# Paced weight swaps: 16 loads per segment tied to steps of TensorE's program

## The chip, the cores and the metric

The kernel runs on one core of one Trainium2 chip. The metric is the device time of one execution in microseconds, taken as the median of several runs. The engines are TensorE (PE, with its weight loads as PEld), VectorE (DVE), ScalarE (ACT), GpSimd (POOL) and SyncE (SP). SyncE computes nothing here; it issues almost all transfers, one after the other, in the order of its own program, and a transfer that has to wait holds up all that stand behind it on that queue.

## What is computed

Two parts are added with a gate per token. Part A is a recurrent attention over 64 segments of 32 tokens with 8 memory rows; part B is a gated feed-forward layer. Cut to the core:

```python
# x: (1, 2048, 640) bf16; H = 32 heads of Dh = 192; M = 8 memory rows; seg_len = 32
for s in range(64):
    h = concat([mem, x[32 * s:32 * s + 32]])            # 40 rows
    q, k, v = h @ Wq, h @ Wk, h @ Wv                    # 640 -> 32 x 192 each
    p = softmax(mask(q @ k.T * Dh ** -0.5))
    o = (p @ v) @ Wo                                    # 6144 -> 640
    mem, a[s] = o[:8], o[8:]
b = (gelu(x @ w_gate) * (x @ w_up)) @ w_down
out = g * a + (1 - g) * b                               # g = sigmoid(sum(x * gate_w))
```

Segment s + 1 needs the memory rows that segment s makes at its very end, so the segments follow one another strictly, and in each all four weight matrices are used once.

## The kernel before

**Tiles and stages.** Part B comes first, in four blocks of 512 tokens (about the first 170 us); then come the 64 segments. In a segment the 32 heads are worked in four *octets* of eight heads. Weights lie in the on-chip memory as *pieces*: a piece of Wq, Wk or Wv is one of five slices of the contraction (k = 0 to 4) for one octet, 128 rows of 3072 bytes, 384 KB; a piece of Wo is one pair of heads' pairs, 128 rows of 3840 bytes, 480 KB. A segment reads 60 pieces of the first sort and 16 of Wo.

**What does not fit is swapped.** All four matrices together are larger than the memory, so 16 slots hold two pieces in turn: 13 slots hold a Q, K or V piece of octet 0 or of octet 3 (`partner`, NSQ = 13), three hold a Wo piece of the first or of the last pairs (NSW = 3). Even segments go through the octets 0, 1, 2, 3, odd ones 3, 2, 1, 0. So a slot's first piece is read at the start of a segment, and its other piece has to be there toward the end of the same segment; the next segment then starts with what lies there. The 16 loads of a segment thus have a window from the read that frees the slot to the read of the other piece. One further piece of Q (k = 2) is read from a copy, and its slot is loaded at a fixed step late in the segment.

**The order of the work is written out by hand.** `PROG0` to `PROG3` (from L528) list the steps of a segment for s % 4 = 0, 1, 2, 3, called its *kind* below. `("g", n, k)` is a step of projections: slice k of the pieces of group n (L1152, and L226 for a piece that goes with the same loaded rows). Group 0 reads Q and K of the segment's first octet, group 1 its V and the second octet's Q and K, and so on; groups 3, 4 and 5 read Q, K and V of the last octet. `("sc", i)` are scores (mask at L1201), `("ex", i)` softmax, `("pt", i)` the transposes of P, `("pv", i)` P times V (L1296, L1298), `("wo", i, j)` the output projection (L1352 and L1378; L1397 in segments of kind 3), `("lf", ...)` and `("le", ...)` projections of the last 8 rows of four later segments, made ahead (L944), and `("vb", k)` V of such rows.

**Who issues what.** `segment(s)` (L1476) walks through the list; after each step it calls `swap_loads` (L664, called at L1529). That function takes the keys of the pieces just read, and for each that has a partner adds the partner's load to SyncE's program at once (`load_piece`, L647; its transfers show as L649), with a wait on the last reader of the slot. K pieces of slices 2 and 3 of the first group are held until the Q pieces of slices 3 and 4 have been added. After `swap_loads`, at fixed steps, the small transfers are added to the same queue:

- at ("g", 0, 3): the store of left rows of an earlier segment (L955); in kind 0 also the out store of the last segment (`out_store`, L1043)
- at ("g", 1, 4): in kinds 1 to 3 the out store; in all the load of the next segment's x (L757); in kind 0 four stores of left rows into the output (`outl_store`, L1086), in kind 2 four loads into the same buffer (`bzl_load`, L1038)
- in kind 1, at the first ("le", ...): the store of the first half of left rows (`mid_store`, L1433)
- at ("wo", 0, 1): in kind 1 the second half of those rows (L1433); the load of part B's rows (`bz_load`, L1032), which waits until the out store has landed; in kind 1 also a load of left x (`xl_load`, L761)
- at ("pv", 2): two staging loads of left rows (`stg_load`, L1019; in kind 1 the second is issued later), the load of the Q piece with k = 2, and in kinds 0 and 2 four more of L1086 or L1038.

`_Sched.add` (L73) finds each operation's dependencies from the memory regions that it reads and writes; an out store and a left-row store of the same segments write overlapping rows of the output, so the later one waits for the earlier one's landing.

Of the kernel before, what the change touches and what calls it, by code (L numbers as in the profile page):

```python
# [238 lines left out]
def _build(nc, A_x, A_mem0, A_Wq, A_Wk, A_Wv, A_Wo, seg_len, w_gate, w_up, w_down,  # L239
# [34 lines left out]
    S_ = _Sched(nc)  # L274
# [238 lines left out]
    def piece_src(key):  # L513
        if key[0] == 3:
            return Wo2[:, key[1]]
        m, o_, k = key
        return (Wq2, Wk2, Wv2)[m][:, k, OW * o_:OW * (o_ + 1)]
# [4 lines left out]
    def piece_view(key, o):  # L522
        if key[0] == 3:
            return bview(o, GO).rearrange("p (c n) -> p c n", n=Dm)
        return bview(o, GQ)

    GROUPS = [[(0, 0), (1, 0)], [(2, 0), (0, 1), (1, 1)], [(2, 1), (0, 2), (1, 2)], [(2, 2), (0, 3)], [(1, 3)], [(2, 3)]]
# [46 lines left out]
    def octet(s, i):  # L574
        return i if s % 2 == 0 else NOCT - 1 - i
# [67 lines left out]
    later = []  # L643

    loaded = {}

    def load_piece(key, name):  # L647
        loaded[slot_id[key]] = key
        S_.add("sp", lambda e: e.dma_start(piece_view(key, res_off[key]), piece_src(key)), writes=[r_res[key]],  # L649
               dma_sem="slot%d" % slot_id[key], name="%s %s" % (name, key))  # L650

    def piece(seg, key):
        order = orders[seg % 4]
        oi = last_req.get(seg, -1) + 1
        assert order[oi] == key, "pieces must be consumed in order"
        last_req[seg] = oi
        if seg == 0 and key in tmp_off:
            return left_piece(key)
        if seg and key == (EM, octet(seg, 0), EK):
            return None, None  # L660
        done_keys.append(key)
        return piece_view(key, res_off[key]), r_res[key]

    def swap_loads(seg, item):  # L664
        if item[:2] == ("g", 0) and EK <= item[2] < KT - 1:
            later.extend(key for key in done_keys if key[0] == 1)
            done_keys[:] = [key for key in done_keys if key[0] != 1]
        elif later:
            done_keys[:] = sorted(done_keys + later, key=lambda key: key[:1] + key[2:])
            del later[:]  # L670
        for key in done_keys:
            other = swap_in.get(key)
            if other is None or (other in partner) == (seg % 2 == 0):
                continue
            load_piece(other, "swap s%d" % seg)
        del done_keys[:]

    def left_piece(key):
        if key in tmp_off:
            return piece_view(key, tmp_off[key]), r_tmp[key]  # L680
        return piece_view(key, res_off[key]), r_res[key]
# [448 lines left out]
    def proj(s, item):  # L1130
# [25 lines left out]
        for n, (m, i) in enumerate(group_at(item)):  # L1156
            o, bk = octet(s, i), bk_of[(m, i)]
            g_, rg_ = piece(s, (m, o, k))
            S_.add("pe", mms(m, bk, htile(k), k, g_, n > 0),
                   reads=([rg_] if rg_ else r_ek) + [r_Hm[int(k >= KA[1])], r_HxT], writes=[r_ps[bk]],  # L1160
                   name="%s s%d o%d k%d" % ("QKV"[m], s, o, k))
# [206 lines left out]
    def wo_part(s, item):  # L1368
        ub = item[1] % NUB
        u = uT[ub]  # L1370
        pairs = wo_pairs(s, item)
        lasto = item[1] == NOCT - 1
        allp = wo_pairs(s, ("wo", NOCT - 1)) if lasto else [p for i in range(NOCT - 1) for p in wo_pairs(s, ("wo", i))]
        held = [(p,) + piece(s, (3, p)) for p in pairs]
        if lasto:
            for p, g_, rg_ in held:
                for c in range(3):
                    S_.add("pe", [lambda e, j=j, c=c, g_=g_, p=p: e.matmul(  # L1378
                        ps[32 * j:32 * j + 32, OB2, SC:512], u[:, p % 4, c, 0:L], g_[:, c, DJ * j:DJ * (j + 1)],
                        start=(p == allp[0] and c == 0), stop=(p == allp[-1] and c == 2),  # L1380
                        tile_position=(0, 32 * j)) for j in range(4)],
                        reads=[rg_, r_uTh[p % 4 // 2]], writes=[r_ps[OB2]], name="Wo s%d p%d" % (s, p))
            return
        for (pa, ga, ra), (pb, gb, rb) in zip(held[::2], held[1::2]):
            for c in range(3):
                S_.add("pe", wo_split(OB, [u[:, pa % 4, c, 0:L], u[:, pb % 4, c, 0:L]], [ga[:, c, :], gb[:, c, :]],
                                      pa == allp[0] and c == 0, pb == allp[-1] and c == 2),
                       reads=[ra, rb, r_uT[ub]], writes=[r_ps[OB]], name="Wo s%d p%d" % (s, pa))
        if pairs[-1] == allp[-1]:
            half_copy(OB, "s%d" % s)  # L1390

    def wo_both(s, item):
        for p in wo_pairs(s, item):
            g_, rg_ = piece(s, (3, p))
            u, ru = (U3h[p % 4 // 2][:, p % 2], r_U3h[p % 4 // 2]) if item[1] == NOCT - 1 else (U3[:, p % 4], r_U3)
            for c in range(3):
                S_.add("pe", [lambda e, i=i, g_=g_, c=c, p=p, u=u: e.matmul(  # L1397
                    ps[64 * i:64 * i + 64, LB, 0:2 * DJ], u[:, c, :], g_[:, c, 2 * DJ * i:2 * DJ * (i + 1)],
                    start=(p == NWP - 1 and c == 0), stop=(p == 0 and c == 2), tile_position=(0, 64 * i),
                    skip_group_check=True) for i in range(2)],  # L1400
                    reads=[rg_, ru], writes=[r_ps[LB]], name="Wb s%d p%d" % (s, p))
# [74 lines left out]
    def segment(s):  # L1476
# [3 lines left out]
        for n, item in enumerate(PROGS[q]):  # L1480
# [43 lines left out]
            else:  # L1524
                if q == 3:
                    wo_both(s, item)
                else:
                    wo_part(s, item)
            swap_loads(s, item)  # L1529
            if item == ("g", 0, KT - 2):  # L1530
                for x in to_store:
# [109 lines left out]
def bass_gated_mix__memory_aug_recurrent_mem_tr__glu_gated_geglu__prompt_kernel(  # L1641
    nc,
    A_x,
    A_mem0,
    A_Wq,
    A_Wk,
    A_Wv,
    A_Wo,
    A_seg_len,
    B_x,  # L1650
    B_w_gate,
    B_w_up,
    B_w_down,
    gate_w,
    out,
):
    _build(nc, A_x, A_mem0, A_Wq, A_Wk, A_Wv, A_Wo, A_seg_len, B_w_gate, B_w_up, B_w_down, gate_w, out)
# [33 lines left out]
```

## Time and profile before

| | us |
|---|---|
| median of three runs | 1701.26 |
| lowest, highest | 1691.61, 1701.76 |
| the profiled execution | 1693.53 |
| its span, first to last instruction | 1691.8 |
| TensorE busy | 1555.9 |
| VectorE, ScalarE, GpSimd busy | 985.0, 780.1, 549.0 |
| all transfers | 499.30 MB |

The span is what the trace shows of the profiled execution; times of rows are counted from its start. In the profile's rows a group of instructions is named by its line, engine, operation, what it writes and reads, and its count; then come busy time and mean of one, and the idle time of the engine just before, with what ended most of it. In a row of the timeline stand start, duration, engine, line, operation, and in brackets idle time before it. The on-chip memory is one tile, `arena`, and the accumulators one, `ps`, so rows are told apart by their lines and by the matrix that a transfer reads. An issue row of SyncE gives when the issue began and how long issuing took, for several issues of one line together if they follow each other; how long a transfer takes to land is a separate answer.

### The profile page before, as it was taken

How to read it: one execution, taken by the hardware profiler on the slowest of the kernel's cores; microseconds unless marked ns; L12 is line 12 of the kernel's file. 1: busy time of each engine (PE TensorE's matmuls, PEld its weight loads, DVE VectorE, ACT ScalarE, POOL GpSimd, SP SyncE). 2: the span in 40 equal slices, each digit the busy share in tenths (PEclk: the TensorE clock that was granted, in tenths of full speed). 3: DMA queues.
4: the chain of work that ended last, by engine and by line, in shares of the span. 5: the costliest groups of instructions: out<-in, count | busy, mean ns of one | idle time of the engine just before them, and what ended most of it. 6: DMA issues, size and time to landing. Idle time of an engine off the chain costs nothing.

```text
span 1691.8 us, 76086 instructions
## 1 busy us (share of the span) xinstructions
PE 1555.9 (92%) x37107; PEld 775.0 (46%) x28147; DVE 985.0 (58%) x3039; ACT 780.1 (46%) x1890; POOL 549.0 (32%) x1625
## 2 busy tenths in 40 slices
PE   9999989999989989899999899898989899898986
PEld 4444345444444445454444444454534444454443
DVE  6452656666555656566665656555665556565663
ACT  2222444544445554455444554444544445445442
POOL 1100233333333333333333333333333333233332
PEclk9999999999999999999999999999999999999998
DMA  9915988988889898889889897889888898889895
GB/s 297 334 47 161 356 293 308 331 311 290 306 298 328 298 325 298 304 314 327 305 291 324 290 338 277 305 296 317 312 296 311 281 330 295 278 297 320 300 329 188
DMA packets 275418, 499.30 MB, mean 295 GB/s; under 512 B 121119, under 2 KB 136327, under 8 KB 275079
## 3 DMA queue, kind: packets, MB, share of 16 engines
q1 hardware_dynamic: 271000, 491.30, 83.5%
q8 instruction: 255, 4.18, 1.0%
q10 hardware_dynamic: 4079, 3.14, 0.6%
q14 instruction: 84, 0.69, 0.1%
HBM read 473.25 MB, written 21.09 MB: 292 GB/s over the span
## 4 chain that ended last, share of the span: by engine, by line
PE 62%; DMA 28%; SPq 4%; DVE 3%; issue 2%; ACT 1%; POOL 0%; DVEq 0%; ACTq 0%; POOLq 0%
PE ps L1152 18%; PE ps L226 16%; DMA arena<-in_A_Wo_dram 13%; DMA arena<-in_A_Wk_dram 11%; PE ps L1397 7%; PE ps L1352 4%; DMA arena<-in_A_Wv_dram 4%; PE ps L1296 3%; PE ps L944 2%; PE ps L1201 2%; PE ps L1378 2%; SPq L649 2%; PE ps L853 2%; PE ps L850 2%; PE ps L876 1%
## 5 line engine op out<-in xcount | busy, mean ns | idle before, releaser
L1152 PE MATMUL ps<-arena 128*32 128x384 bf16 x8640 | 653.9, 331 | 35.2 <-DMA arena<-in_A_Wk_dram 15.9
L226 PE MATMUL ps<-arena 128*32 128x384 bf16 x8960 | 642.2, 329 | 0.4 <-ACT arena L1173 0.2
L1152 PEld LDWEIGHTS ps<-arena 128*32 128x32 bf16 x8640 | 227.6, 97 | 417.6 <-issue 270.6
L1190 DVE STREAM_TRANSPOSE arena<-arena 128x384 bf16<-128x384 bf16 x512 | 273.5, 559 | 56.1 <-ACT arena L1173 55.2
L1173 ACT ACTIVATE arena<-ps 128x384 bf16<-128x384 f32 x512 | 230.1, 492 | 109.5 <-PE ps L1152 109.2
L1176 ACT ACTIVATE arena<-ps 128x384 bf16<-128x384 f32 x256 | 125.2, 489 | 183.2 <-PE ps L1152 181.0
L1352 PE MATMUL ps<-arena 128*32 128x320 bf16 x3456 | 179.7, 302 | 13.4 <-issue 8.9
L1228 DVE TENSOR_REDUCE arena<-ps 104x4 f32<-104x160 f32 x256 | 82.8, 323 | 183.1 <-PE ps L1216 183.0
L1193 POOL COPY arena<-arena 64x160 bf16<-64x160 bf16 x256 | 81.3, 318 | 255.6 <-DVE arena L1190 248.3
L1026 POOL COPY arena<-arena 128x96 bf16<-128x96 bf16 x256 | 69.3, 271 | 273.4 <-PE ps L1216 190.3
L1334 ACT ACTIVATE arena<-ps 128x480 bf16<-128x480 f32 x192 | 109.7, 571 | 99.0 <-PE ps L1298 99.0
L1281 ACT ACTIVATE arena<-ps 128x448 bf16<-128x448 f32 x192 | 105.2, 548 | 59.8 <-PE ps L1268 58.9
L1240 ACT ACTIVATE ps<-ps 104x160 f32<-104x160 f32 x256 | 74.1, 290 | 107.5 <-DVE ps L1230 107.5
L1296 PE MATMUL ps<-arena 128*64 128x160 bf16 x1536 | 117.8, 241 | 2.9 <-issue 2.9
L1425 ACT ACTIVATE arena<-ps 128x384 bf16<-128x384 f32 x120 | 57.2, 491 | 135.1 <-PE ps L944 85.5
L1397 PE MATMUL ps<-arena 128*64 128x320 bf16 x1536 | 118.4, 303 | 1.0 <-issue 0.3
L1352 PEld LDWEIGHTS ps<-arena 128*32 128x32 bf16 x3456 | 91.1, 96 | 59.3 <-ACT arena L1275 15.1
L944 PE MATMUL ps<-arena 128*32 128x384 bf16 x1280 | 113.1, 334 | 5.6 <-issue 5.5
L1378 PE MATMUL ps<-arena 128*32 128x160 bf16 x2304 | 61.1, 236 | 55.9 <-DMA arena<-in_A_Wo_dram 38.2
L1242 DVE TENSOR_REDUCE arena<-ps 104x4 f32<-104x160 f32 x256 | 79.3, 310 | 56.5 <-ACT ps L1240 52.5
L1342 POOL COPY arena<-arena 128x96 bf16<-128x96 bf16 x192 | 51.3, 267 | 180.3 <-ACT arena L1324 99.7
L1298 PE MATMUL ps<-arena 128*64 128x64 bf16 x1536 | 103.1, 193 | 2.4 <-issue 2.4
(102 smaller groups left out, 2377.6 us busy)
## 6 DMA issues: line engine op xcount, KB each, us to landing
arena<-in_A_Wk_dram SPq DMA_DIRECT2D x335, 384.0 KB, 6.1
arena<-in_A_Wv_dram SPq DMA_DIRECT2D x335, 384.0 KB, 8.5
arena<-in_A_Wo_dram SPq DMA_DIRECT2D x205, 480.0 KB, 5.9
arena<-in_A_Wq_dram SPq DMA_DIRECT2D x209, 384.0 KB, 5.5
arena<-left_qk_scratch SPq DMA_DIRECT2D x126, 96.0 KB, 5.2
left_qk_scratch<-arena SPq DMA_DIRECT2D x49, 192.0 KB, 5.2
left_qk_scratch<-arena SPq DMA_DIRECT2D x30, 96.0 KB, 5.3
ffn_b_scratch<-arena ACTq DMA_DIRECT2D x16, 160.0 KB, 4.1
```

The lines of the kernel that those rows point to most:

```text
L226: return e.add_instruction(mybir.InstMatmult(name=nm, start_tensor_calc=like["start"], stop_tensor_calc=stop, tile_size=(128, 32), tile_po ...
L944: fns.append(lambda e, outp=outp, rhs=rhs, j=j: e.matmul(outp, lhs, rhs, start=(k == 0), stop=(k == KT - 1), tile_position=(0, 32 * j)))
L1152: fns.append(lambda e, outp=outp, rhs=rhs, j=j: e.matmul(outp, lhs, rhs, start=(k == 0), stop=(k == KT - 1), tile_position=(0, 32 * j)))
L1173: S_.add("act", lambda e, m=m, bk=bk: e.activation(out=rows_sb[m], in_=ps[:, bk, 0:384], func=ACTF.Copy), reads=[r_ps[bk]], writes=[r_rows ...
L1176: S_.add("act", lambda e, i=i, bk=bk: e.activation(out=v_sb[i % NVB].rearrange("p (c n) -> p c n", c=3), in_=ps[:, bk, 0:384].rearrange("p ...
L1190: S_.add("dve", lambda e: e.transpose(out=dst[:, :, 0:L], in_=rows_sb[m].rearrange("p (c r) -> p c r", r=L)), reads=[r_rows[m]], writes=[r ...
L1281: S_.add("act", lambda e: e.activation(out=PT, in_=ps[:, bank, 0:PTW + 128], func=ACTF.Copy), reads=[r_ps[bank]], writes=[r_PT], name="pT ...
L1296: return [lambda e: e.matmul(full, v[:, e0:e0 + 64], PTm[:, i], start=True, stop=False, tile_position=(0, 64 * i), skip_group_check=True), ...
L1298: lambda e: e.matmul(part, vl[:, e0:e0 + 64], PTl[:, i], start=False, stop=True, tile_position=(0, 64 * i), skip_group_check=True)]
L1334: S_.add("act", lambda e: e.activation(out=apx(u[:, 0, 0, :], [[rs, na], [3 * rs, 4], [1, R]]), in_=ps[:, A, 0:na * W].rearrange("p (c t r ...
L1352: fns.append(lambda e, i=i, t=t, j=j, gv=gv: e.matmul(ps[32 * j:32 * j + 32, bank, 0:2 * DJ].rearrange("p (h n) -> p h n", h=2), lhs2[i], ...
L1397: S_.add("pe", [lambda e, i=i, g_=g_, c=c, p=p, u=u: e.matmul(ps[64 * i:64 * i + 64, LB, 0:2 * DJ], u[:, c, :], g_[:, c, 2 * DJ * i:2 * DJ ...
```

## The change

The load of a swap is no longer added to SyncE's program in the step that frees its slot. `swap_loads` puts the partner on a list, `pend`. A counter, `clock[0]`, adds up an assumed cost of TensorE for every step (`item_ns`: 162 ns for a piece of projections, 470 for scores, 500 for P times V, 405 for a step of the output projection, 810 in kind 3, and so on). After each step loads are taken from the list as long as the counter has reached `clock[1]`, the time that the next one is due; each load moves that time on by SPACE = 950 ns, though never further back than one such space behind the counter. So after a pause two loads can go out together, and then one per 950 ns of assumed cost. Each load gets one more dependency: the newest operation in TensorE's program at that point. A piece that is still on the list when it is to be read is loaded at once, together with those ahead of it. The small transfers keep their steps, and the load of the Q piece with k = 2 does too.

```diff
+    pend, clock, SPACE = [], [0, 0], 950
...
     def piece(seg, key):
...
+        while key in pend:
+            next_load(seg)
         done_keys.append(key)
...
     def swap_loads(seg, item):
...
-            load_piece(other, "swap s%d" % seg)
+            pend.append(other)
         del done_keys[:]
+        clock[0] += item_ns(seg, item)
+        while pend and clock[0] >= clock[1]:
+            next_load(seg)
+
+    def next_load(seg):
+        load_piece(pend.pop(0), "swap s%d" % seg)
+        S_.streams["sp"][-1].deps.add(S_.streams["pe"][-1])
+        clock[1] = max(clock[1], clock[0] - SPACE) + SPACE
+
+    def item_ns(seg, item):
+        q = seg % 4
+        if item[0] == "g":
+            return 162 * (len(GROUPS[item[1]]) + int(q == 0 and any(m == 2 and i for m, i in GROUPS[item[1]])))
+        if item[0] == "lf":
+            return 325 if item[1] == q else 0
+        if item[0] == "wo":
+            return 810 if q == 3 else 405
+        return {"sc": 470, "pv": 500, "pt": 100, "vb": 162}.get(item[0], 0)
```

## The prediction

> **What bounds the kernel now.** I read the page first, then the groups by line, then the four kinds of segment by windows, then SyncE's queue beside TensorE inside them.
>
> ```profile
> span 1691.8 us, 76086 instructions
> PE 1555.9 (92%) x37107; PEld 775.0 (46%) x28147; DVE 985.0 (58%) x3039; ACT 780.1 (46%) x1890; POOL 549.0 (32%) x1625
> PE 62%; DMA 28%; SPq 4%; DVE 3%; issue 2%; ACT 1%; POOL 0%; DVEq 0%; ACTq 0%; POOLq 0%
> ```
>
> TensorE is busy for 92%, yet 28% of the chain that ended last is DMA. So two resources share the end: TensorE idles about 136 us (1691.8 - 1555.9), and part of that is weights that came late:
>
> ```profile
> L1152 PE MATMUL ps<-arena 128*32 128x384 bf16 x8640 | 653.9, 331 | 35.2 <-DMA arena<-in_A_Wk_dram 15.9 <-DVE arena L1597 8.0 <-DMA arena<-in_A_Wv_dram 4.5
> L1378 PE MATMUL ps<-arena 128*32 128x160 bf16 x2304 | 61.1, 236 | 55.9 <-DMA arena<-in_A_Wo_dram 38.2 <-issue 8.7 <-ACT arena L1324 5.4
> ```
>
> The last number but one of each pair of bars is the idle time before the group. Waits on weights are 15.9 + 4.5 + 38.2 = 58.6 us, about 0.9 us for each of 64 segments, most of it on the output projection at a segment's end (L1378). By windows, one segment of each kind (segments 24 to 27, s % 4 = 0 to 3):
>
> ```profile
> 737.41:760.83 23.42, 21.99 (x612) 11.28 (x473) 15.21 (x49) 11.18 (x28) 7.95 (x24) 1.00 0.85 299
> 760.83:784.68 23.85, 21.33 (x593) 10.02 (x433) 14.53 (x47) 12.01 (x31) 7.57 (x24) 1.00 0.88 304
> 784.68:806.74 22.06, 20.30 (x553) 9.40 (x413) 13.36 (x45) 11.84 (x29) 8.00 (x25) 1.00 0.92 332
> 806.74:829.50 22.76, 21.94 (x508) 12.21 (x388) 13.28 (x43) 11.12 (x30) 9.86 (x28) 1.00 0.88 316
> ```
>
> Columns: length, busy PE, PEld, DVE, ACT, POOL, granted clock, DMA share, GB/s. The clock is full. DMA share 0.85 to 0.92 beside TensorE's 0.90 to 0.96 means that what moves in the DMA queue moves the segment.
>
> **The change part by part.** In a segment 13 pieces of 384 KB and 3 of 480 KB are swapped. I call them K0 to K4, Q3, Q4, V0 to V4 and Wo a, b, c. SyncE's queue in segment 24 after K0 and K1, and below it the times from issue to landing of K0, Q3, Q4, K3 and K4 (the x3 row is K2, K3, K4):
>
> ```profile
> 738.78 0.33 SPq L649 DMA_DIRECT2D arena<-in_A_Wq_dram  x1
> 739.15 0.58 SPq L1043 DMA_DIRECT2D out_dram<-arena  x1
> 739.77 0.47 SPq L649 DMA_DIRECT2D arena<-in_A_Wq_dram  x1
> 740.29 1.38 SPq L649 DMA_DIRECT2D arena<-in_A_Wk_dram  x3
> 741.71 2.83 SPq L649 DMA_DIRECT2D arena<-in_A_Wv_dram  x5
> 744.59 0.44 SPq L757 DMA_DIRECT2D arena<-x_scratch  x1
> 745.13 2.40 SPq L1086 DMA_DIRECT2D out_dram<-arena  x4
> ...
> arena<-in_A_Wk_dram SPq DMA_DIRECT2D x1, 384.0 KB, 3.2
> arena<-in_A_Wq_dram SPq DMA_DIRECT2D x1, 384.0 KB, 4.2
> arena<-in_A_Wq_dram SPq DMA_DIRECT2D x1, 384.0 KB, 5.4
> arena<-in_A_Wk_dram SPq DMA_DIRECT2D x1, 384.0 KB, 6.4
> arena<-in_A_Wk_dram SPq DMA_DIRECT2D x1, 384.0 KB, 6.9
> ```
>
> Thirteen swaps are issued within 7 us and then queue: K3 (issued 740.8) lands at 747.2, K4 (741.2) at 748.1, one piece per 1.0 us, while the first one, on an empty queue, takes 3.2 us. Landing is set by the bytes ahead, not by the issue.
>
> *Pacing itself: 0.* By the diff's own step costs, in a segment of kind 0 the first nine projection steps are 5 x 324 + 4 x 486 = 3564 ns, where K2 goes out; one more and the first scores (486 + 470) make 4520, K3; the next step (648) 5168, K4; V4 goes out at 10.3 us, after the first P·V, instead of about 4. A piece needs to be issued 3.2 us before it could land in the old order, and V4 lands behind twelve others of 1.0 us, past 15 us. So the steps alone starve nothing; the cover is the backlog of two to five pieces, and it is 1 to 2 us deep. No swap is left pending at its use, so the forced issue in `piece` does not act. The added wait on TensorE's newest instruction costs SyncE some tenths, under the same cover.
>
> What does move is everything else on SyncE's queue, because those small transfers are issued at fixed steps and now stand **ahead of** 5 to 7 swaps instead of behind them.
>
> *(1) Kind 0, a new block of the queue.* Before K3 now come the x load and four stores of left rows (L1086: 2.40 us of issue). The first of those stores waits until the previous out store (L1043) has landed, as both write the same output rows. In the row above it is issued at 745.13, long after; in the new order SyncE comes to it at about 742. The out store lands behind Q3 (738.78 + 4.2 = 743.0) and at least one piece's 1.0 us before Q4 (739.77 + 5.4 = 745.2), so in 743.0 to 744.2; I take the middle, 743.6. SyncE is free at 743.6 + 2.4 = 746.0, and K3 is issued 5.3 us later than before. By then Q4 and K2 have landed (745.2, 746.2), the queue is empty, and K3 pays the empty-queue 3.2: 749.3, K4 750.3, V0 751.3, V1 752.3. TensorE reads them here:
>
> ```profile
> 749.35 1.00 PE L1152 MATMUL ps<-arena 128*32 128x384 bf16 x20
> 750.70 0.51 PE L1152 MATMUL ps<-arena 128*32 128x384 bf16 x8
> 751.44 0.50 PE L1152 MATMUL ps<-arena 128*32 128x384 bf16 x8
> ```
>
> The x20 row is K0 to K4, five steps of 0.16, so K4 is read at 750.0; V0 at 750.7, V1 at 751.4. Stalls: K4 0.3; V0 751.3 - 751.0 = 0.3; V1 752.3 - 752.0 = 0.3; 0.9 in all. With the out store at 743.0 it is 0.25 (V1 alone), at 744.2 1.45. Where TensorE already waits for the last Wo piece at the end, part is given back; I take 0.6. The Trainium skill's "DMA: Bandwidth & Descriptors" (section "Anatomy of one DMA — SWDGE (gpsimd) path") fits a transfer as 2.0 us plus bytes over 436 GB/s, an estimate of 2.9 us for 384 KB; this queue is SyncE's and the row says 3.2, so the row is used. By the page's 2.9 the landings are 0.3 earlier, K4's stall goes, this term would be 0.6 instead of 0.9, and the sum some 4 us lower.
>
> *(2) Kind 1, the third Wo piece.* It becomes due 0.12 us of step cost after its slot is free, so it is issued one step later, behind the second left store, the bz load and the xl load that belong to the earlier step. In segment 25:
>
> ```profile
> 775.46 2.59 SPq L649 DMA_DIRECT2D arena<-in_A_Wo_dram  x3
> 778.10 0.55 SPq L1433 DMA_DIRECT2D left_qk_scratch<-arena  x1
> 779.32 0.72 SPq L761 DMA_DIRECT2D arena<-left_x_scratch  x1
> ...
> arena<-in_A_Wo_dram SPq DMA_DIRECT2D x1, 480.0 KB, 5.9
> left_qk_scratch<-arena SPq DMA_DIRECT2D x1, 96.0 KB, 6.7
> arena<-left_x_scratch SPq DMA_DIRECT2D x1, 40.0 KB, 5.7
> ...
> 782.25 0.45 PE L1378 MATMUL ps<-arena 128*32 128x160 bf16 x13 [1.00 <-DMA arena<-in_A_Wo_dram]
> 783.57 0.39 PE L1378 MATMUL ps<-arena 128*32 128x160 bf16 x12 [0.87 <-DMA arena<-in_A_Wo_dram]
> ```
>
> The third Wo piece (issued 777.62) lands at 783.5 and TensorE starts on it at once, after 0.87 of idling: nothing covers this. The store lands at 784.8 and the xl load at 785.0, so 1.5 us of landings now come ahead of it. Part of that is skew between the engines' tails that stays; the store is 96 KB, a quarter of a 1.0 us piece, and the two loads 80 KB together, so at least 0.5. I take 1.2, nearer the landings. In kinds 0, 2 and 3 only the 40 KB bz load comes ahead of it, 0.1 us, inside the waits above.
>
> *(3) Kind 2: 0.* Two things cancel. For: in kind 1 the second staging load waits for the landing of that left store and holds up the next segment's first swaps,
>
> ```profile
> SPq L1019 <- DMA left_qk_scratch<-arena: 58.2, 15, 5.0
> 793.98 2.62 SPq L1038 DMA_DIRECT2D arena<-ffn_b_scratch  x4
> ```
>
> 3.9 us each (58.2/15); with the store earlier and the segment's end later, kind 2 starts on a free queue, about 0.4 earlier. Against: out store, x load and four bzl loads (2.62 us of issue) now come ahead of K3. They wait for nothing, so K3 goes out near 8 us into the segment, and 3.2 more is 11.3 against an uncovered need near 11.8. Between -0.5 and +0.7.
>
> *(4) Kind 3.* Out store and x load come ahead of K4, on which TensorE already waits:
>
> ```profile
> 818.59 0.35 PE L1152 MATMUL ps<-arena 128*32 128x384 bf16 x4 [0.26 <-DMA arena<-in_A_Wk_dram]
> ```
>
> They are 70 KB, 0.2 of a piece: 0.25, between 0.2 and 0.7 (a store among pieces may cost more than its bytes).
>
> *(5) Gains elsewhere.* bz, out and x land some 6 us earlier. GpSimd and VectorE read them at a segment's end, beside TensorE's output projection, and no TensorE wait names them: 0. If the cover were gone it would be a gain.
>
> *(6) The first segment.* Five resident Wo pieces are issued at a fixed step that V4's swap now comes after: 5 x 1.2 = 6 us later, but the segment's end waits for Wo anyway: +1.
>
> Sum: 0.6 + 1.2 + 0 + 0.25 = 2.05 per four segments, times 15 (the first and the last lack some of the transfers) = 31, plus 1 = 32. The profiled execution took 1693.5 (span 1691.8): 1693.5 + 32 = 1725.5. The median of the runs shown, 1701.3, is 7.8 above it, the lowest, 1691.6, 1.9 below; I keep **1725**.
>
> **The rivals.** *Faster: lighter queue, faster transfers.* With two or three pieces outstanding instead of ten, each might move quicker and the tails of the sixteen engines draw together. Decisive is whether landings come closer than 1.0 us apart. Then K4 in kinds 2 and 3 and the Wo pieces arrive before TensorE: half of the 58.6 us of waits is 29, so 1664. Against: the queue is full of the same bytes until V4, and the first piece, alone in the queue, still took 3.2. The Trainium skill, same page, "Latency and other measured facts", gives HBM access as 0.2 us on average and 2 us at high load, with a smaller fixed cost at lighter load; by that rule this rival gains a little. Chance 0.17.
>
> *No change: hidden.* The out store lands at 743.0, and of (2) only the bytes count, 0.5: (0.25 + 0.5 - 0.3 + 0.2) x 15 = 10, so 1704. For: the DMA totals stay. Chance 0.25.
>
> *Slower still: starving feeds itself.* Issue follows TensorE and TensorE waits for pieces; a block of SyncE late in kind 0 delays the Wo issue too. All upper ends: 1.45 + 1.5 + 0.7 + 0.7 = 4.35 x 15 = 65, plus 4 at the start: 1763. Chance 0.13.
>
> *That it doesn't do what it says:* in the places where DMA is full until V4, later issue changes no landing; that is the second rival.
>
> **How the numbers follow.** The forecast, 1711 to 1745, has 0.45. The range reaches from 1690, which leaves out most of the faster case, to 1765. About 1% (17 us, 1684 to 1718) is what a measurement of this kernel can tell from no change. Slower: 0.45 + 0.13 = 0.58, with the forecast's own lower edge against the hidden case's upper; within 1% 0.25; faster 0.17.
>
> **What would show it.** (1) In kind 0, SyncE waits at L1086's store (its new line) for out_dram, some 1.5 us, and idle before K4, V0, V1 by Wk and Wv grows by 0.6 to 0.9 a segment. (2) In kind 1 the last L1378 wait on Wo grows from 0.9 to about 2. (3) L1019's wait on the left store shrinks from 3.9. (4) The wait for K4 in kind 3 grows by 0.25. bz's waits for out_dram vanish in kinds 2 and 3. Wrong it would be if pieces land closer than 1.0 us apart, if the Wo waits shrink, or if K3 in kind 0 is issued before 8 us into the segment.

## The result and the profile after

| | before | after |
|---|---|---|
| median of 4 runs, us | 1698.75 | 1801.43 |
| lowest to highest | 1691.61 to 1701.76 | 1799.2 to 1802.83 |
| ratio, 95% interval | | 1.061 [1.057, 1.065] |
| span of the profiled execution | 1691.8 | 1797.5 |

The change costs 103 us. The forecast was 1725 with a range to 1765: the direction held, the size did not. The page of the changed kernel, its first two lines and the shares of the chain:

```profile
span 1797.5 us, 76069 instructions
PE 1593.0 (89%) x37090; PEld 776.6 (43%) x28147; DVE 985.9 (55%) x3039; ACT 781.6 (43%) x1890; POOL 549.5 (31%) x1625
...
PE 61%; DMA 34%; DVE 2%; issue 1%; SPq 1%; ACT 0%; POOL 0%; DVEq 0%; POOLq 0%; ACTq 0%
```

DMA's share of the chain went from 28% to 34%. The 105.7 us of span fall into two parts. TensorE's idle time (span less busy) went from 135.9 to 204.5 us: 68.6. And TensorE is *busy* 37.1 us longer with the same matmuls, which no row of the prediction had a term for. The waits of TensorE on weights, by the view of waits (in all, times, longest):

```profile
PE ps L1173 <- DMA arena<-in_A_Wk_dram: 51.1, 70, 2.3
PE ps L1173 <- DMA arena<-in_A_Wv_dram: 48.5, 61, 4.5
PE ps L1399 <- DMA arena<-in_A_Wo_dram: 48.0, 46, 2.4
```

They were 15.9, 4.5 and 38.2. So the new waits are at the K and V pieces in the middle of a segment, much less at the Wo pieces of its end. The same four segments as before (24 to 27, kinds 0 to 3), by windows:

```profile
776.73:804.41 27.68, 24.33 (x613) 12.12 (x474) 15.29 (x49) 11.33 (x28) 7.96 (x24) 0.88 0.74 253
804.41:829.30 24.89, 21.51 (x592) 9.93 (x432) 14.46 (x47) 12.22 (x31) 7.95 (x24) 1.00 0.85 297
829.30:855.70 26.40, 22.32 (x552) 9.58 (x412) 13.28 (x45) 11.83 (x29) 7.95 (x24) 0.94 0.80 273
855.70:879.22 23.52, 22.12 (x509) 12.15 (x389) 13.33 (x44) 11.16 (x30) 9.59 (x27) 1.00 0.87 304
```

Kinds 0 and 2 grew most (23.42 to 27.68, 22.06 to 26.40); their DMA share fell to 0.74 and 0.80, and the granted clock, the column before it, to 0.88 and 0.94. Means over segments 8 to 59, taken between the first projections of neighbouring segments, are the better measure:

| kind | before | after | difference |
|---|---|---|---|
| 0 | 23.88 | 26.56 | +2.68 |
| 1 | 24.67 | 24.83 | +0.16 |
| 2 | 22.91 | 25.26 | +2.34 |
| 3 | 22.74 | 23.89 | +1.15 |

*Kind 0, segment 24.* SyncE's queue from the out store on:

```profile
778.61 0.58 SPq L1064 DMA_DIRECT2D out_dram<-arena  x1
779.54 0.33 SPq L650 DMA_DIRECT2D arena<-in_A_Wq_dram  x1
780.52 0.33 SPq L650 DMA_DIRECT2D arena<-in_A_Wk_dram  x1
780.89 0.43 SPq L778 DMA_DIRECT2D arena<-x_scratch  x1
783.64 2.40 SPq L1107 DMA_DIRECT2D out_dram<-arena  x4
786.08 1.48 SPq L650 DMA_DIRECT2D arena<-in_A_Wk_dram  x2
787.61 2.81 SPq L650 DMA_DIRECT2D arena<-in_A_Wv_dram  x5
```

After the x load SyncE stands still until 783.64, when the out store has landed; then come the four stores and only then K3, 9.35 us into the segment (by the prediction some 8.6). Issue to landing of K3 alone, and of K4 with K3 (median of the two):

```profile
arena<-in_A_Wk_dram SPq DMA_DIRECT2D x1, 384.0 KB, 3.2
...
arena<-in_A_Wk_dram SPq DMA_DIRECT2D x2, 384.0 KB, 3.9
```

K3 takes the 3.2 us of an empty queue, as predicted. K4 takes 4.5, which is why the two have 3.9 together. And TensorE waits where it reads K4 and V0:

```profile
791.10 0.35 PE L1173 MATMUL ps<-arena 128*32 128x384 bf16 x4 [1.38 <-DMA arena<-in_A_Wk_dram]
...
793.91 0.83 PE L1173 MATMUL ps<-arena 128*32 128x384 bf16 x8 [1.87 <-DMA arena<-in_A_Wv_dram]
```

From K3's landing (786.08 + 3.2 = 789.3) to K4's it is 1.7 us and from there to V0's 2.8, not 1.0. Over the segments of kind 0 from 8 to 59 the three spacings from K3 to V1 are 1.31, 1.91 and 1.38 in the mean, 4.6 together; in the kernel before they were 1.25, 1.00 and 0.98, 3.2 together. (The medians are 0.99, 1.88 and 1.01, since it differs from segment to segment which one is long.) The windows between those landings (last three columns: granted clock, DMA share, GB/s):

```profile
786.90:789.33 2.43, 2.43 (x74) 1.34 (x60) 1.70 (x7) 1.88 (x4) 1.05 (x4) 1.00 0.73 207
789.33:791.06 1.73, 0.35 (x7) 0.10 (x4) 1.45 (x6) 0.28 (x1) 0.39 (x2) 1.00 0.98 350
791.06:793.87 2.81, 0.94 (x16) 0.55 (x16) 0.58 (x1) 1.06 (x2) 1.09 (x2) 0.58 0.96 354
```

207 x 2.43 + 350 x 1.73 + 354 x 2.81 = 2103 KB were moved in these 7 us, 5.3 pieces of 393 KB, while three landed. So the queue moves bytes at full rate again soon, but a piece is complete only when the last of its sixteen shares is. The trace records these sixteen completions: 15 of V0's had come by 792.29, the last came at 793.87, when 15 of V1's and 9 of V2's had come too. In the segments of kind 0 the first and the last share of K3, K4, V0 and V1 lie 0.57, 0.89, 1.55 and 1.98 us apart in the median. In the kernel before, with its backlog, they lie 1.7 to 2.0 apart on each of the four. So on a full queue the lag is the same from piece to piece and the landings follow 1.0 apart; after the pause it starts small and grows, and its growth (1.98 - 0.57 = 1.4) comes on top. The Trainium skill's "DMA: Bandwidth & Descriptors" (section "Why a DMA increments its semaphore by 16 and not by 1") states the ground of this: the engines finish independently and only the full count means that all has landed. The trace agrees, by V0's sixteenth share, 1.58 us after the fifteenth.

*Kind 2, segment 26.*

```profile
835.02 0.60 SPq L1064 DMA_DIRECT2D out_dram<-arena  x1
835.66 0.47 SPq L778 DMA_DIRECT2D arena<-x_scratch  x1
836.17 2.46 SPq L1059 DMA_DIRECT2D arena<-ffn_b_scratch  x4
838.68 0.92 SPq L650 DMA_DIRECT2D arena<-in_A_Wk_dram  x2
...
843.01 0.35 PE L1173 MATMUL ps<-arena 128*32 128x384 bf16 x4 [0.85 <-DMA arena<-in_A_Wk_dram]
843.99 0.35 PE L1173 MATMUL ps<-arena 128*32 128x384 bf16 x4 [0.63 <-DMA arena<-in_A_Wk_dram]
```

Nothing waits here, but 3.66 us (835.02 to 838.68) of issuing stand ahead of K3, which goes out 9.38 us into the segment, and TensorE idles for K3, for K4 and later for two V pieces.

*The clock.* Windows of 3.41 us, the length of the clock's records, around the stalls of segment 24:

```profile
788.13:791.54 3.41, 2.00 (x56) 1.02 (x50) 2.43 (x8) 1.50 (x5) 0.85 (x3) 1.00 0.91 311
791.54:794.95 3.41, 1.54 (x28) 0.89 (x28) 0.58 (x1) 1.02 (x2) 1.09 (x2) 0.50 0.98 371
794.95:798.37 3.42, 3.42 (x74) 2.05 (x68) 0.62 (x2) 0.54 (x1) 0.51 (x1) 0.50 0.65 233
798.37:801.78 3.41, 3.41 (x100) 2.26 (x88) 1.75 (x7) 1.89 (x5) 1.06 (x3) 1.00 1.00 338
```

In the first window TensorE is busy 2.00 of 3.41 us; the next runs at half clock. In that one it is busy 1.54; the next runs at half clock too, though TensorE is busy throughout; then the clock is full again. Summed over the clock records of the trace, half clock was granted for 41.6 us before and for 113.7 us after. 72.1 us more at half speed are 36 us of extra work time, and 37.1 is what TensorE's busy time grew by.

### The profile page after: what moved, and what is told of

Same layout as the page of the kernel before. It is cut to its first block, busy times and chain, and to the rows that moved or that the text cites. A ratio compares the mean times of both kernels' runs of the same rounds, so it can differ in the third digit from the quotient of the medians.

```text
span 1797.5 us, 76069 instructions
## 1 busy us (share of the span) xinstructions
PE 1593.0 (89%) x37090; PEld 776.6 (43%) x28147; DVE 985.9 (55%) x3039; ACT 781.6 (43%) x1890; POOL 549.5 (31%) x1625
## 4 chain that ended last, share of the span: by engine, by line
PE 61%; DMA 34%; DVE 2%; issue 1%; SPq 1%; ACT 0%; POOL 0%; DVEq 0%; POOLq 0%; ACTq 0%
PE ps L226 17%; PE ps L1173 17%; DMA arena<-in_A_Wo_dram 16%; DMA arena<-in_A_Wv_dram 10%; DMA arena<-in_A_Wk_dram 7%; PE ps L1418 5%; PE ps L1373 4%; PE ps L874 3%; PE ps L871 2%; PE ps L965 2%; PE ps L1222 2%; PE ps L1317 2%; PE ps L897 2%; PE ps L1399 1%; PE ps L1230 1%
## 5 line engine op out<-in xcount | busy, mean ns | idle before, releaser
L1173 PE MATMUL ps<-arena 128*32 128x384 bf16 x8640 | 671.7, 336 | 111.8 <-DMA arena<-in_A_Wk_dram 51.1
L226 PE MATMUL ps<-arena 128*32 128x384 bf16 x8960 | 646.0, 332 | 0.4 <-ACT arena L1194 0.4
L1373 PE MATMUL ps<-arena 128*32 128x320 bf16 x3456 | 184.0, 314 | 7.8 <-issue 4.3
L965 PE MATMUL ps<-arena 128*32 128x384 bf16 x1280 | 112.2, 339 | 0.8 <-issue 0.8
```

What stands on the lines that cost most here:

```text
L226: return e.add_instruction(mybir.InstMatmult(name=nm, start_tensor_calc=like["start"], stop_tensor_calc=stop, tile_size=(128, 32), tile_po ...
L965: fns.append(lambda e, outp=outp, rhs=rhs, j=j: e.matmul(outp, lhs, rhs, start=(k == 0), stop=(k == KT - 1), tile_position=(0, 32 * j)))
L1173: fns.append(lambda e, outp=outp, rhs=rhs, j=j: e.matmul(outp, lhs, rhs, start=(k == 0), stop=(k == KT - 1), tile_position=(0, 32 * j)))
L1373: fns.append(lambda e, i=i, t=t, j=j, gv=gv: e.matmul(ps[32 * j:32 * j + 32, bank, 0:2 * DJ].rearrange("p (h n) -> p h n", h=2), lhs2[i], ...
```

## The experiments

The theories were *order* (the small transfers now ahead of K3 to V1 make pieces late; the first expectations call it 'block'), *third Wo piece* (the same at the segment's end), *pacing* (the wait on TensorE or the spacing itself) and *clock* (stalls are paid twice). All times stand beside runs of the kernel before on the same chip. The last column sums the clock records of the profiled run.

| kernel | median us | ratio to before, 95% | half clock us |
|---|---|---|---|
| small transfers late | 1749.0 | 1.031 [1.026, 1.037] | 99.8 |
| order without the wait on TensorE | 1765.3 | 1.041 [1.036, 1.047] | 119.7 |
| kind 0's stores late | 1762.9 | 1.038 [1.031, 1.044] | 109.5 |
| fillers in kinds 0 and 2 | 1792.9 | 1.057 [1.051, 1.063] | 72.0 |
| kind 2's loads late | 1767.1 | 1.041 [1.036, 1.047] | 82.1 |
| Wo not paced | 1776.7 | 1.048 [1.044, 1.053] | 99.6 |
| small late, Wo not paced | 1720.1 | 1.016 [1.009, 1.022] | 75.9 |
| only Wo paced | 1716.4 | 1.012 [1.009, 1.015] | 78.8 |
| only Wo paced, filler | 1702.8 | 1.007 [1.004, 1.010] | 34.0 |
| kind 2's loads on ScalarE's queue | 1770.9 | 1.047 [1.043, 1.051] | 130.0 |
| before, left-row store late | 1678.0 | 0.991 [0.988, 0.994] | 50.9 |
| before, filler | 1704.4 | 1.007 [1.004, 1.011] | 39.0 |
| SPACE 0 | 1705.6 | 1.005 [1.002, 1.009] | 65.9 |
| SPACE 475 | 1706.0 | 1.005 [1.003, 1.008] | 52.0 |

**Small transfers late.** Those of ("g", 1, 4) are added once the list of swaps is empty:

```diff
+            if not pend:
+                for x in small:
+                    x()
+                del small[:]
...
-                    out_store(s - 1)
+                    small.append(lambda: out_store(s - 1))
```

and the same for `x_load`, `outl_store` and `bzl_load` at that step.

> Pacing kept, but the small transfers of step ("g",1,4) (out store of kinds 1 to 3, x load, the four left-row stores of kind 0, the four bzl loads of kind 2) are added to SyncE's queue only when the list of pending swaps is empty, that is behind V4 as before. Theory 'block' (the small transfers now ahead of K3 empty the transfer queue in kinds 0 and 2): the stalls on K3 to V1 go, 1700 to 1720 us. Theory 'pacing' (the wait on TensorE and the spacing of 950 ns leave too little queued, whatever stands between): 1770 us or more.

1749, between the two. Half of the loss is gone, and the waits on K and V are down to 14.2 and 12.4 us (before: 15.9 and 4.5). But the wait on Wo grew:

```profile
PE ps L1399 <- DMA arena<-in_A_Wo_dram: 76.1, 61, 2.9
PE ps L1173 <- DMA arena<-in_A_Wk_dram: 14.2, 27, 1.7
PE ps L1173 <- DMA arena<-in_A_Wv_dram: 12.4, 28, 3.9
```

The Wo wait went from 48.0 to 76.1. SyncE late in segment 26 of this kernel, of kind 2 (it begins at 813.25), from the bzl loads on, TensorE at the last Wo piece, and SyncE's wait in front of the bz load over the whole run, in this kernel (L1053) and in the kernel before (L1032):

```profile
826.71 2.43 SPq L1059 DMA_DIRECT2D arena<-ffn_b_scratch  x4
829.19 1.32 SPq L650 DMA_DIRECT2D arena<-in_A_Wo_dram  x2
831.86 0.58 SPq L1053 DMA_DIRECT2D arena<-ffn_b_scratch  x1
832.49 0.48 SPq L650 DMA_DIRECT2D arena<-in_A_Wo_dram  x1
...
837.57 0.39 PE L1399 MATMUL ps<-arena 128*32 128x160 bf16 x12 [2.36 <-DMA arena<-in_A_Wo_dram]
...
SPq L1053 <- DMA out_dram<-arena: 52.2, 31, 3.0
SPq L1032 <- DMA out_dram<-arena: 53.4, 30, 3.2
```

The third Wo piece stands behind the bz load, which itself waits for the out store to land (nothing is issued from 830.5 to 831.86), and TensorE idles 2.36 us for it. The kernel before has the same wait, but there the three Wo pieces are issued ahead of it. So part of the 3.1% is made by the late out store and the paced Wo pieces together, and this run alone does not give the price of the order. The prediction had in kind 2 only the 40 KB of the bz load ahead of the third Wo piece.

**Order without the wait.** The line that makes a load depend on TensorE's newest operation is left out.

```diff
-        S_.streams["sp"][-1].deps.add(S_.streams["pe"][-1])
```

> The order of the queue as in the changed kernel, but the added wait on TensorE's newest instruction is left out, so SyncE runs ahead as soon as a slot is free. Theory 'block': the store of left rows in kind 0 still waits for the out store to land, so K3 still goes out some 8 us into a segment of kind 0; in kind 2 the bzl loads now run a little earlier: 1755 to 1790 us. Theory 'pacing': 1700 to 1720 us.

1765, as *order* said. By kinds: +2.23, +0.51, +2.22, +0.20, against the table's +2.68, +0.16, +2.34, +1.15. The order alone makes nearly all of kinds 0 and 2.

**One kind at a time.** `outl_store` or `bzl_load` alone deferred, by the first diff.

> Only kind 0's four left-row stores are moved back behind V4; everything else as changed. Theory 'block': kind 0 gives back its 2.7 us per segment, times 15 is 40: 1755 to 1770 us, and the stalls of kind 2 stay. Theory 'pacing': 1790 to 1803 us, since the queue is thin without the stores too.

> Only kind 2's four bzl loads are moved back behind V4; everything else as changed. Theory 'order': kind 2 gives back the stalls on K3 to V4, at most its 2.34 us per segment, less what the last Wo piece then takes: 1770 to 1790 us. Rival (bzl loads are harmless, the wait on TensorE makes K3 and K4 late): 1793 to 1803 us.

1763 and 1767: by the ratios 2.3% and 2.0% come back, some 39 and 33 us. Kind 0 falls to 23.85 us in the first (before: 23.88), kind 2 to 23.43 in the second (before: 22.91). In the first, kind 2 grows further, from 25.26 to 25.89.

**Other queue.** Kind 2's four loads issued by ScalarE, at the same step, so that the transfers stay and only SyncE's 2.5 us go.

```diff
-    def bzl_load(g, js):
+    def bzl_load(g, js, eng=AUXQ):
...
-                S_.add(AUXQ, lambda e, j=j, n=n, lo=lo, hi=hi: e.dma_start(
+                S_.add(eng, lambda e, j=j, n=n, lo=lo, hi=hi: e.dma_start(
...
-                    bzl_load(g, js)
+                    bzl_load(g, js, "act" if js[0] == 0 else AUXQ)
```

> As changed, but kind 2's four bzl loads at ("g",1,4) are issued by ScalarE's queue instead of SyncE's, at the same step. Theory 'issue time' (they cost because SyncE spends 2.6 us issuing them while no weight piece follows): kind 2 gives back most of its 2.3 us per segment, 1765 to 1780 us, as when they were moved behind V4 (1767). Rival (the transfers themselves hold up the pieces, or the wait on TensorE does): 1793 to 1803.

1771, as expected. SyncE in segment 26 (begins at 826.39):

```profile
830.56 0.60 SPq L1064 DMA_DIRECT2D out_dram<-arena  x1
831.20 0.47 SPq L778 DMA_DIRECT2D arena<-x_scratch  x1
831.71 0.91 SPq L650 DMA_DIRECT2D arena<-in_A_Wk_dram  x2
```

K3 goes out 5.3 us into this segment instead of 9.4; over all segments of kind 2 the median is 7.0 instead of 8.5 (5.7 with the loads behind V4). TensorE's idle time in kind 2 falls from 3.58 to 2.25 us per segment (before: 1.92). So most of the waiting in kind 2 comes from SyncE's time to issue and not from the loads' bytes. The segment itself falls only from 25.26 to 24.14, because half clock stayed: 130.0 us of it in this run, the most of all kernels here.

**Wo.** Wo pieces loaded at once in the changed kernel; the same with the small transfers late; and the reverse, only Wo paced. The diff of the first, and of the last:

```diff
             pend.append(other)
+            if other[0] == 3:
+                load_piece(pend.pop(), "swap s%d" % seg)
```

```diff
             pend.append(other)
+            if other[0] < 3:
+                load_piece(pend.pop(), "swap s%d" % seg)
```

> As changed, but the three Wo pieces are loaded as soon as their slots are free, not paced. By the prediction's second term (1.2 us in each segment of kind 1) 18 us come back: 1783. Theory 'order and third Wo piece': in the changed kernel TensorE is already late when Wo is due, so the idle time before the last Wo piece grew by only 0.36 in kind 1 and 0.26 in kind 2: 1785 to 1797 us.

> The small transfers behind V4 as before, and Wo not paced; so SyncE's order is that of the kernel before, and only the 13 Q, K and V swaps keep their wait on TensorE. Theory 'third Wo piece' (what was left with the small transfers moved back is the third Wo piece standing behind bz, left-row and bzl transfers): 1697 to 1712 us. Rival 'pacing' (the spacing of 950 ns thins the queue): 1735 to 1752 us.

> The kernel before with the three Wo pieces of a segment paced and the 13 others loaded at once. Theory 'third Wo piece': 1735 to 1752 us, with idle time before the last Wo piece of 1.5 to 2 us in kinds 1 and 2. Rival 'pacing': 1697 to 1712 us.

The first stands at 1.048 for the changed kernel's 1.061, 1.3% or some 21 us, nearer to the prediction's 18 than to the other expectation. The two others split what was left: 1720 without the Wo pacing, 1716 with it alone, so neither *third Wo piece* nor *pacing* holds it alone, and both expectations missed. They nearly add up: 1.6% and 1.2% against the 3.1% of the kernel with both.

Taken in this order, the 6.1% of the change divide as follows: 1.3% for pacing Wo (6.1 against 4.8), 3.2% for the small transfers ahead of the swaps (4.8 against 1.6, both with Wo not paced), and the 1.6% that is left for pacing the 13 other swaps.

**The wait or the spacing.**

> The changed kernel with SPACE = 0 instead of 950: every load goes out at the step that frees its slot, so SyncE's order is that of the kernel before, and only the added wait on TensorE's newest instruction is left. If that wait costs part of the 26 us that the 13 paced swaps took with the old order: 1705 to 1722 us. If the spacing of 950 ns (K3 to V4 issued up to 4 us later) is the cause: 1690 to 1702 us.

> The changed kernel with SPACE = 475. In kind 2 the out store, x load and bzl loads stand ahead of V2 to V4 only, in kind 0 ahead of fewer pieces too, and these are needed 3 us after K3. If the loss comes from small transfers standing ahead of K3 to V1: 1700 to 1725 us. If the loss grows with the spacing as such: about half of 104, 1740 to 1755 us.

SPACE = 0 keeps the wait on TensorE and the old order: 0.5%, some 9 us, the price of the wait. With 475 the loss is no larger, 0.5%. So it does not grow in step with the spacing: between 475 and 950 it jumps from 0.5% to 6.1%, when the small transfers come to stand ahead of K3 to V1 and not of the later V pieces only. The spacing of 950 is not free in itself: with the old order and Wo not paced, 1.6% were left.

**The clock.** Matmuls with zero weights, added into the bank that is being summed, in front of the read on which TensorE waits. In the changed kernel, in front of K4 (with K3 as the moving data) and of V0 (with K4):

```diff
+            nf = {(0, 4): 4, (0, 5): 4, (2, 4): 4, (2, 5): 2}.get((s % 4, item[1]), 0) if s and (item[1], k) in ((4, 4), (5, 0)) else 0
+            if nf:
...
+                S_.add("pe", [lambda e, x=x, j=j, bk=bk, fg=fg: e.matmul(
+                    ps[32 * j:32 * j + 32, bk, 0:384], elw[:, 0:2, :].rearrange("p a b -> p (a b)"), fg[:, 384 * j:384 * (j + 1)],
+                    start=(k == 0 and x == 0), stop=False, tile_position=(0, 32 * j)) for x in range(nf) for j in range(4)],
```

> The changed kernel with matmuls of zero weights added in front of K4 (4 pieces' worth, some 0.65 us) and V0 (4 in kind 0, 2 in kind 2), accumulated into the same bank, so that TensorE works where it stood still; the output is the same. Theory 'clock' (windows of 3.4 us in which TensorE was half idle are followed by 3.4 or 6.8 us at half clock, and that is a third of the loss): half-clock time falls from 114 us to under 70, the time to 1765 to 1790 us. Rival (the half clock follows something else, or the stalls set the end alone): half-clock time stays over 100 us and the time is 1797 to 1812 us, the fillers being pure extra work.

Half clock fell from 113.7 to 72.0 us: of the six half-idle windows that began 11 to 14 us into segments of kind 0 and halved the clock, none is left. But the ratio went only from 1.061 to 1.057, inside both intervals, and the expected time was missed. An explanation, not tested, is that where the next piece is late anyway a faster TensorE waits for it. The trace of the changed kernel has a comparison, though not a test, since segments with longer stalls are the ones that get half clock: of its 13 segments of kind 0 from 8 to 59, the six with half clock in them took 27.74 us in the mean, the seven without 25.54, and 1.5 of these 2.2 us are TensorE's busy time. The same in front of the last Wo piece of kind 1 (12 times 4 matmuls of 160 columns), with only Wo paced and in the kernel before:

> The kernel with only the Wo pieces paced, with matmuls of zero weights (12 times 4, some 0.9 us at full clock) in front of the last Wo piece in segments of kind 1, where 12 of its 18 half-clock periods begin; the output is the same. Theory 'clock' (most of what Wo pacing costs, 1716 against 1694, is the half clock after that wait): half-clock time from 79 to about 35 us, the time 1696 to 1708 us. Rival (the wait itself is the cost): half-clock time may fall, the time stays at 1712 to 1722.

> The kernel before with the same zero-weight matmuls in front of the last Wo piece of kind 1, where 8 of its 11 half-clock periods begin. Theory 'clock': half-clock time from 42 to about 15 us, the time 1680 to 1690 us. Rival: 1692 to 1700 us.

With only Wo paced: half clock from 78.8 to 34.0 us, the time from 1716.4 to 1702.8, the ratio from 1.012 to 1.007. That is in the range of *clock*, but the intervals overlap a little. In the kernel before it failed: half clock 41.6 to 39.0, and 11 us slower; segments of kind 1 grew from 24.67 to 25.44. Why the halvings stayed there was not settled.

**A faster version.** In the kernel before, kind 1's first left-row store is put off behind the three Wo pieces:

```diff
-            (mid_store if m == 0 else mid_later.append)((g, o, m, dst, rd))
+            mid_later.append((g, o, m, dst, rd))
```

> The kernel before with one more transfer put off: in kind 1 the first half of left rows is stored at the step of the second half, behind the three Wo pieces instead of ahead of them. If the 96 KB ahead of Wo delay the last Wo piece, on which TensorE idles 1.39 us there: 0.6 to 1.0 us less in each of 15 segments, 1680 to 1688 us. If the landing of Wo is set by the pieces alone: 1691 to 1697, or slower, since the staging load after it waits for that store.

```profile
775.78 2.14 SPq L649 DMA_DIRECT2D arena<-in_A_Wo_dram  x3
777.96 1.27 SPq L1433 DMA_DIRECT2D left_qk_scratch<-arena  x2
...
PE ps L1378 <- DMA arena<-in_A_Wo_dram: 18.6, 36, 1.1
```

1678.0, 0.991 [0.988, 0.994]: faster than both. The waits on Wo halve, from 38.2 to 18.6 us, and segments of kind 1 fall from 24.67 to 23.32. It is the mechanism of the prediction's second term, backwards: a store that stands ahead of a Wo piece makes TensorE wait.

## Why the prediction was wrong, and where it was right

By the table of kinds, times 15, the sum was 31 us short in kind 0, 35 in kind 2 and 14 in kind 3, and 16 too high in kind 1. So the terms that failed are (1), too small, and (3), put at nothing; half clock had no term at all.

*Pacing itself, 0: nearly.* The wait alone costs some 9 us (SPACE 0), and with 950 the 13 paced swaps in the old order cost 26. "The steps alone starve nothing" is nearly so: the mean idle time before any of K3 to V4 was 0.61 us at most in that kernel (K3 in kind 3). The 26 us lie in kinds 2 and 3, which take 23.91 and 23.52 instead of 22.91 and 22.74. A likely part of it, read from the trace and not tested, is that V4's late issue moves the transfers behind it into the Wo pieces' way: kind 2's first Wo piece goes out at 15.5 us in the median instead of 13.4.

*(1) Kind 0: right mechanism, size off by four.* The block formed as described. SyncE waits for the out store 1.8 us per segment (23.8/13; the row that the prediction named):

```profile
SPq L1107 <- DMA out_dram<-arena: 23.8, 13, 2.5
SPq L1040 <- DMA left_qk_scratch<-arena: 33.0, 15, 2.9
```

The failing step is "K3 pays the empty-queue 3.2: 749.3, K4 750.3, V0 751.3, V1 752.3". K3 paid 3.2 (3.25 in the median), after an issue 0.5 us later than forecast (9.1 us into the segment for 8.6). But the pieces behind it did not follow 1.0 apart: from K3 to V1 it took 4.6 us in the mean and not 3.0. The 1.0 was read on a queue with a backlog, where the shares of every piece are spread equally wide; after the pause the spread grows from 0.57 to 1.98 us, piece by piece. Stalls were 2.46 us on K4, V0 and V1 in the mean (0.89, 1.13, 0.44), not the 0.9 of which the prediction kept 0.6, and half clock followed in six of 13 segments.

*(2) Kind 1: the size right by luck, the place wrong.* 1.2 x 15 = 18 us were forecast; taking the Wo pacing away gives some 21 back, and alone it costs 1.2%, some 20. The third Wo piece does wait behind other transfers, but most of the cost is not in kind 1. There idle time before the third Wo piece grew from 1.34 to 1.75 in the mean, while that before the second of the three fell from 0.52 to 0.14, and the segment grew by 0.16. In kinds 2 and 3 idle time before the third piece grew by 0.26 and 0.34, where the prediction had it "inside the waits above", and when Wo is not paced kind 1 gives back 0.11 and the other three kinds 0.65, 0.30 and 0.52.

*(3) Kind 2, 0: wrong.* K3 was put "near 8 us", which was 9.4 in segment 26 and 8.5 in the median, and it was compared with K3's own need only. K3 then took 3.6 us in the median, and K4, needed 0.2 us after it, landed 1.3 after it in the mean: TensorE idled 0.29 us for K3, 0.95 for K4 and 0.28 for V0. The gain that should cancel it came (L1040's wait, 58.2/15 = 3.9, is now 33.0/15 = 2.2) and saved nothing in kind 2's middle. The term was +2.3, times 15 some 35 us: the largest error.

*(4) Kind 3: +1.15 for 0.25.* No experiment took it alone; with the order but without the wait on TensorE it is +0.20, as forecast, so the rest needs the wait too; the wait alone, with SPACE 0, gives +0.46.

*"The clock is full."* It was so in the four segments shown. That stalls of 1 to 2 us would lower it had no term; 37 us of the span. How much of this is time that would go without it is open: the fillers of the changed kernel took 21 us of it away (half of 41.7) and the median fell by 8.5.

The forecast's upper rival, 1763, had the right signs but summed the same undersized terms. The faster rival failed where it was decisive: the shares of K3 did draw together after the pause (0.57 us for 1.7), but no median of the landings came clearly closer than 1.0 apart.

What stays open: which transfer engines lag, and why their lag builds up anew when the queue restarts; the rest of kind 3; and the filler's failure in the kernel before.

## What to carry to other kernels

A transfer that is moved later on an in-order queue changes places with all that is issued at fixed steps: list those that come to stand ahead of it, with their issue time and what they wait for, before asking whether the moved one still arrives. On a queue that has run empty, cost the pieces behind the first by landings after a pause, not by the spacing of a backlog. Where stalls leave a window half idle, look for half clock after it as a second cost; how much of it comes back when the window is filled was not the same here from kernel to kernel (0.5% with only Wo paced, within the noise in the changed kernel, nothing in the kernel before).

## What the hardware showed

A window of 3.41 us in which TensorE was busy for 2.00 was followed by half clock, with no single gap above 1.4 us in it. The Trainium skill's "TensorE: Matmul & The Clock Gate" (section "HAM oscillation — how this bites in real kernels") gives as its rule no idle gaps above some 3.4 us. By the traces here that is too mild: in the changed kernel, between 194 and 1640 us, 20 windows at full clock with a busy share of 0.23 to 0.59 were followed by half clock, none with a larger share was, and some between 0.45 and 0.59 were not. A window at half clock was followed by a second one at busy shares up to 0.70, and not from 0.80 on.
